# A copy moved to ScalarE's DMA queue, and one more step between the words of a 64-bit unit and their join

## The chip, the cores and the metric

One core of one Trainium2 chip runs the whole program. The metric is the device time in microseconds (us); several runs of the same kernel are given by their median. Engines are named as the profile names them: PE is TensorE's matmuls and PEld its weight loads, DVE is VectorE, ACT is ScalarE, POOL is GpSimd, and SP is SyncE, which here does nothing but issue DMAs. Each of these engines takes its instructions in the order of its own queue; an instruction that waits holds up whatever stands behind it on the same engine.

## The reference

```python
def rmsnorm(x, g):
    return x / np.sqrt(np.mean(x * x, axis=-1, keepdims=True) + 1e-06) * g
# q, k, v: (4, 12, 448, 64) float32, 4 batches of 12 heads
scores = scale * rmsnorm(q, g_q) @ rmsnorm(k, g_k).T
attn = exp(scores - max(scores)); attn = attn / (sum(attn) + 1e-09)
x = (attn @ v), heads joined -> (1792, 768)
h = x @ w_in;  r = maximum(h, 0);  x = (r * r) @ w_out            # 768 -> 2048 -> 768
h = ((x @ w1) * (x @ w2)) @ w3;    out = h @ w_out2               # 768 -> 1024 -> 1024 -> 768
```

The six weight matrices arrive as 64-bit floats, while q, k and v arrive as 32-bit floats.

## The kernel before

**Precision and units.** Every product is made from two parts, a rounded value (`hi`) and what is left of it (`lo`), so one product of two tiles takes three matmuls (lines 262 to 264, function `mm3`). Weights are handled in units of 128 x 384 or 128 x 512 elements. A 64-bit unit is loaded as pairs of 32-bit words into a `raw64` tile; `words` makes of them a scaled high word on ACT (line 194) and a low word on POOL or ACT (lines 200 and 198), both in place; `join` on DVE (line 207) puts the two together as 32-bit floats in a `raw` tile; `split_hi` copies the rounded part on ACT (line 106) and `split_lo` takes the rest on POOL or DVE (line 114), into an `hl` tile that PE reads. In the trace `raw64` and `raw` have the same name, raw.

**Which units are 64-bit.** There are 120 of them: 32 for `w3` and the last matrix, whose product `w3o` is made first, and 88 for `w_in`, `w_out`, `w1` and `w2`, while batch 0 passes through the network. When such a unit has been joined it is also stored to DRAM (line 215); batches 1 to 3 load that 32-bit copy (line 183) and have neither words nor joins.

**Stages.** The heads are worked one after another, 12 to a batch. Between the pieces of a head's attention the program fills in matmuls of another job (`fill`): the product `w3o` while heads 0 to 11 run (to about 186 us), the network on batch 0 while heads 12 to 23 run (186 to about 465 us), the network on batches 1 and 2 during the last 24 heads (to about 1029 us), and the network on batch 3 alone at the end.

**Order around the units.** `advance(u)` moves the pipeline on by one unit. In the step of unit i it loads up to unit i + `LOAD64_AHEAD`, stores what has been joined, forms words up to i + `WORD_AHEAD`, joins up to i + `JOIN_AHEAD`, copies the rounded part of i + 1 and takes the rest of i. A `raw64` tile has 4 buffers, so the load of a unit waits until the unit four before it has been joined. All of these loads and stores are issued on SP.

**Order around the probabilities.** `stage_exp(h, s)` makes two of the four row blocks of a head's probabilities with two exponentials on ACT (line 543). For heads 12 and above the 112 x 896 result `p` is then copied from SBUF to SBUF by a DMA into `pw`, a tile of the type that PE's transposes (line 570, `stage_t`) read; this copy (line 549) is issued on SP, two copies a head, 72 in all. `stage_t(h, ...)` runs after the next head's first scores and needs both copies. `pw` has 3 buffers. ACT issues DMAs of its own already: the 24 stores of the output (line 379). The order in which an engine's instructions stand is fixed when the program is built and need not be that of the source: in the trace an output store is issued behind the ACT instruction that follows it in the source.

Of the kernel before, what the change touches and what calls it, by code (L numbers as in the profile page):

```python
# [8 lines left out]
F32 = mybir.dt.float32  # L9
F32R = mybir.dt.float32r  # L10
U16 = mybir.dt.uint16
U32 = mybir.dt.uint32
# [17 lines left out]
def attention_moe_kernel(  # L30
# [15 lines left out]
    nc = tc.nc  # L46
# [26 lines left out]
    PACE = (1.17, 0.93, 1.08, 0.64)  # L73
    HI_AHEAD = 1
    JOIN_AHEAD = 2
    WORD_AHEAD = 3
    LOAD32_AHEAD = 3
    LOAD64_AHEAD = 5

    const = ctx.enter_context(tc.tile_pool(name="const", bufs=1))  # L80
    xp = ctx.enter_context(tc.tile_pool(name="x", bufs=8))
# [7 lines left out]
    t3 = ctx.enter_context(tc.tile_pool(name="t3", bufs=3))  # L89
# [81 lines left out]
    def is64(i):  # L171
        return units[i][0].dtype != F32

    def load_next():
        i = pos["load"]
        src = units[i][0]
        n = src.shape[-1]
        if is64(i):
            t = t3.tile([128, 512, 2], U32, name="raw64", tag="raw64", bufs=4)
            nc.sync.dma_start(out=t[:, :n, :], in_=src.bitcast(U32).rearrange("p (n t) -> p n t", t=2))  # L180
        else:
            t = rawp.tile([128, 512], F32, name="raw", tag="raw")
            nc.sync.dma_start(out=t[:, :n], in_=src)
        raws[i] = t
        pos["load"] += 1

    def load_to(i):
        while pos["load"] <= min(i, NU - 1) and is64(pos["load"]):
            load_next()

    def words(i):
        t, n = raws[i], units[i][0].shape[-1]
        hi = t[:, :n, 1].bitcast(F32)
        nc.scalar.activation(out=hi, in_=hi, func=AF.Prelu, scale=2.0**-112, alpha=-(2.0**32))  # L194
        low = t.rearrange("p n t -> p (n t)").bitcast(U16).rearrange("p (n t) -> p n t", t=4)[:, :n, 1]
        low_eng = LOW_ENG[i >= U0]
        if low_eng[i % len(low_eng)] == "a":
            nc.scalar.activation(out=t[:, :n, 0], in_=low, func=AF.Copy, scale=2.0**-13, bias=2.0**-14 - 0.5)
        else:
            nc.gpsimd.tensor_scalar(  # L200
                out=t[:, :n, 0], in0=low, scalar1=2.0**-13, scalar2=2.0**-14 - 0.5, op0=ALU.mult, op1=ALU.add
            )

    def join(i):
        t, n = raws[i], units[i][0].shape[-1]
        f = raws[i] = rawp.tile([128, 512], F32, name="raw", tag="raw")
        nc.vector.scalar_tensor_tensor(  # L207
            out=f[:, :n].bitcast(U32), in0=t[:, :n, 1], scalar=3, in1=t[:, :n, 0],
            op0=ALU.logical_shift_left, op1=ALU.bitwise_or,
        )  # L210

    def store(i):
        dst = units[i][1]
        if dst is not None:
            nc.sync.dma_start(out=dst, in_=raws[i][:, :dst.shape[-1]])
# [19 lines left out]
    def upto(what, i, step):  # L235
        while pos[what] <= min(i, NU - 1):
            step(pos[what])
            pos[what] += 1

    def advance(u):  # L240
        while pos["lo"] <= min(u + SPLIT_AHEAD, NU - 1):
            i = pos["lo"]
            for k in range(pos["load"], min(i + LOAD64_AHEAD, NU - 1) + 1):
                if is64(k):
                    load_next()
                elif k <= i + LOAD32_AHEAD and (k <= pos["join"] or not is64(k - 1)):
                    load_next()
                else:
                    break
            upto("store", min(i + JOIN_AHEAD, pos["join"]) - 1, lambda k: is64(k) and store(k))  # L250
            upto("word", i + WORD_AHEAD, lambda k: is64(k) and words(k))
            upto("join", i + JOIN_AHEAD, lambda k: is64(k) and join(k))
            upto("hi", i + HI_AHEAD, split_hi)
            upto("lo", i, split_lo)
# [274 lines left out]
    def stage_exp(h, s):  # L529
        if not (0 <= h < NH):  # L530
            return
        d = heads[h]
        nb, o = d.pop("nb"), d.pop("sc")
        i = h % 2
        if s == 0 and i == 0:
            sums2[h // 2] = small.tile([P, 2, C], F32, name="sm", tag="sm")
        sm = sums2[h // 2]
        c0 = 2 * s
        pp = t3.tile([P, 2, S], F32, name="p", tag="p")
        for j in range(2):  # L540
            c = c0 + j
            p = d["p"][c] = pp[:, j, :]
            nc.scalar.activation(  # L543
                out=p, in_=o[j], func=AF.Exp, scale=d["rq"][:, c:c + 1], bias=nb[:, j:j + 1],
                accum_out=sm[:, i, c:c + 1],
            )
        if h >= H:
            words = t3.tile([P, 2, S], F32R, name="pw", tag="pw")
            nc.sync.dma_start(out=words.bitcast(F32), in_=pp)
            d["p"][c0:c0 + 2] = [words[:, 0, :], words[:, 1, :]]  # L550
        if s == 1 and i == 1:
            nc.vector.tensor_scalar(out=sm, in0=sm, scalar1=1e-9, scalar2=None, op0=ALU.add)
            rs = small.tile([P, 2, C], F32, name="rs", tag="rs")
            nc.vector.reciprocal(out=rs, in_=sm)
            wide = t1.tile([P, C, 2, D], F32, name="rsw", tag="rsw")
            nc.gpsimd.tensor_scalar(
                out=wide, in0=rs.rearrange("p i c -> p c i").unsqueeze(3).to_broadcast([P, C, 2, D]),
                scalar1=1.0, scalar2=1.0, op0=ALU.mult, op1=ALU.mult,
            )
            sums2[h // 2] = wide.rearrange("p c i d -> p c (i d)")  # L560
# [87 lines left out]
    def fill(n):  # L648
# [18 lines left out]
        out=gg, in0=g_sb[:, 0:1], scalar=float(D) ** -0.5, in1=g_sb[:, 1:2], op0=ALU.mult, op1=ALU.mult  # L667
# [8 lines left out]
    for h in range(NH + 1):  # L676
# [5 lines left out]
        stage_qk(h, 0)  # L682
        fill(n)
        stage_exp(h, 0)
        if h % H != 1:
            stage_x(h - 2)
# [12 lines left out]
        stage_qk(h, 1)  # L699
        fill(n)  # L700
        stage_exp(h, 1)
        fill(n)
        stage_v(h - 1)
# [64 lines left out]
```

## Time and profile before

| | |
|---|---|
| median of 3 runs | 1241.29 us (1238.86 to 1243.09) |
| the profiled execution | 1239.56 us, of which the profile's span is 1237.8 us |
| busy share of the span | PE 94%, PEld 85%, DVE 57%, ACT 59%, POOL 63% |
| granted clock of TensorE | 0.986 of full speed over the span |
| DMA | 207.63 MB, mean 168 GB/s; SP's queue 200.92 MB, ACT's 5.51 MB |

A busy share is a mean over stages that differ. The share of the time in which an engine worked has to be read stage by stage, together with what ended each of its waits; the granted clock tells when TensorE ran at half its speed.

### The profile page before, as it was taken

Reading aid. Unit: us, or ns where it says so; the run is one execution under the profiler, and the core shown is the slowest. Engines: PE = TensorE matmul, PEld = TensorE weight load, DVE = VectorE, ACT = ScalarE, POOL = GpSimd, SP = SyncE. Lnnn points to the kernel's source line nnn. Section 1 sums busy time; section 2 is a strip of 40 time slices with the busy share of each in tenths; the row PEclk is TensorE's granted clock in tenths of the full one; section 3 lists DMA queues with packets and bytes.
Section 4 is the critical chain, followed back from the end, with each engine's and each line's share of the span. In section 5 each row is a group of like instructions: output and inputs, shape, how many; then the busy total and the mean of one; then the engine's idle time right before and its main releaser. Section 6 shows DMA issues by size and latency. Waiting matters only on the chain.

```text
span 1237.8 us, 18914 instructions
## 1 busy us (share of the span) xinstructions
PE 1166.3 (94%) x6192; PEld 1054.4 (85%) x6192; DVE 710.7 (57%) x1314; ACT 727.7 (59%) x1553; POOL 784.9 (63%) x772
## 2 busy tenths in 40 slices
PE   3799999898898999999999999999999999999998
PEld 1588887787787888998998998999999999999998
DVE  6699888878888685546567555655664421012110
ACT  5888867667746655655645655656545554443342
POOL 5875434565776756765776664756766556678673
PEclk9899999999999999999999999999999999999999
DMA  6774547787888866455445455454444443433342
GB/s 214 242 227 131 159 140 218 254 272 249 280 259 257 257 192 194 132 155 147 148 127 154 140 155 161 143 154 121 141 138 120 135 136 112 113 109 105 105 120 93
DMA packets 111347, 207.63 MB, mean 168 GB/s; under 512 B 12208, under 2 KB 66704, under 8 KB 111248
## 3 DMA queue, kind: packets, MB, share of 16 engines
q1 hardware_dynamic: 107792, 200.92, 53.8%
q10 hardware_dynamic: 3456, 5.51, 1.2%
q8 instruction: 49, 0.80, 0.3%
q14 instruction: 50, 0.41, 0.1%
HBM read 149.95 MB, written 27.53 MB: 143 GB/s over the span
## 4 chain that ended last, share of the span: by engine, by line
PE 59%; DMA 4%; DVE 4%; ACT 2%; POOL 1%; issue 1%; ACTq 0%; SPq 0%; POOLq 0%; DVEq 0%
PE mm L262 17%; PE mm L264 17%; PE mm L263 17%; PE kv L622 3%; PE pt L570 2%; DMA pw<-p 2%; PE sc L525 1%; PE sc L524 1%; DMA raw<-w 1%; POOL hl L114 1%; ACT p L543 1%; DMA kn<-k_nat 1%; PE kv L508 1%; DVE nb L526 1%; DVE raw L207 0%
## 5 line engine op out<-in xcount | busy, mean ns | idle before, releaser
L114 POOL TENSOR_TENSOR hl<-raw,hl 128x384 fp32r<-128x384 f32 (+1 forms) x383 | 447.0, 1171 | 254.5 <-ACT hl L106 250.9
L106 ACT ACTIVATE hl<-raw 128x384 fp32r<-128x384 f32 (+1 forms) x416 | 233.8, 564 | 146.8 <-PE mm L264 82.0
L262 PE MATMUL mm<-x,hl 128*128 128x448 f32 (+1 forms) x832 | 311.3, 374 | 4.4 <-ACT x L106 1.8
L263 PE MATMUL mm<-x,hl 128*128 128x448 f32 (+1 forms) x832 | 307.2, 369 | 8.1 <-POOL x L114 8.1
L264 PE MATMUL mm<-x,hl 128*128 128x448 f32 (+1 forms) x832 | 306.4, 368 | 3.7 <-DVE hl L114 3.3
L262 PE MATMUL mm<-act,hl 128*128 128x448 f32 (+1 forms) x640 | 238.3, 372 | 0.0
L263 PE MATMUL mm<-act,hl 128*128 128x448 f32 (+1 forms) x640 | 235.7, 368 | 2.3 <-POOL act L114 2.3
L264 PE MATMUL mm<-act,hl 128*128 128x448 f32 (+1 forms) x640 | 235.0, 367 | 0.6 <-POOL hl L114 0.6
L543 ACT ACTIVATE p<-sc,nb,rr 112x448 f32<-112x448 f32 x192 | 137.4, 720 | 82.4 <-DVE nb L527 82.0
L263 PEld LDWEIGHTS mm<-x,hl 128*128 128x128 f32 x832 | 158.5, 190 | 21.9 <-POOL x L114 9.7
L262 PEld LDWEIGHTS mm<-x,hl 128*128 128x128 f32 x832 | 158.4, 190 | 19.6 <-ACT x L106 3.5
L264 PEld LDWEIGHTS mm<-x,hl 128*128 128x128 f32 x832 | 158.6, 191 | 18.3 <-DVE hl L114 4.0
L526 DVE TENSOR_REDUCE nb<-sc 112x1 f32<-112x448 f32 x192 | 113.2, 616 | 34.5 <-PE sc L525 33.0
L263 PEld LDWEIGHTS mm<-act,hl 128*128 128x128 f32 x640 | 122.0, 191 | 12.8 <-POOL act L114 3.6
L200 POOL TENSOR_SCALAR raw<-raw 128x384 uint32<-128x384 uint16 (+1 forms) x110 | 86.3, 785 | 73.3 <-DMA raw<-w_in 25.8
L264 PEld LDWEIGHTS mm<-act,hl 128*128 128x128 f32 x640 | 121.9, 190 | 10.9 <-POOL hl L114 1.3
L262 PEld LDWEIGHTS mm<-act,hl 128*128 128x128 f32 x640 | 122.2, 191 | 9.7 <-ACT act L106 0.2
L114 DVE TENSOR_TENSOR ptr<-pt,ptr 128x448 fp32r<-128x448 f32 x144 | 87.0, 619 | 71.7 <-ACT ptr L106 71.3
L207 DVE SCALAR_TENSOR_TENSOR raw<-raw 128x384 uint32<-128x384 uint32 (+1 forms) x120 | 86.8, 727 | 40.3 <-POOL hl L114 27.2
L114 POOL TENSOR_TENSOR act<-gf,act 128x448 fp32r<-128x448 f32 x80 | 97.8, 1223 | 9.5 <-ACT act L106 5.0
L194 ACT ACTIVATE raw<-raw 128x384 f32<-128x384 f32 (+1 forms) x120 | 70.7, 596 | 52.2 <-DMA raw<-w 19.6
L334 DVE TENSOR_TENSOR gf<-mm,r 128x448 f32<-128x448 f32 x64 | 39.8, 622 | 97.7 <-ACT r L330 97.3
(82 smaller groups left out, 1588.6 us busy)
## 6 DMA issues: line engine op xcount, KB each, us to landing
pw<-p SPq DMA_DIRECT2D x72, 392.0 KB, 4.2
raw<-f_in SPq DMA_DIRECT2D x96, 192.0 KB, 2.4
raw<-f_out SPq DMA_DIRECT2D x72, 256.0 KB, 2.7
raw<-f SPq DMA_DIRECT2D x96, 192.0 KB, 2.4
raw<-w_in SPq DMA_DIRECT2D x32, 384.0 KB, 4.4
raw<-w_out SPq DMA_DIRECT2D x24, 512.0 KB, 6.2
raw<-w SPq DMA_DIRECT2D x32, 384.0 KB, 4.9
raw<-w3o SPq DMA_DIRECT2D x48, 256.0 KB, 2.8
```

Source lines behind the costliest of these rows:

```text
L106: nc.scalar.activation(out=out, in_=in_, func=AF.Copy)
L114: e.tensor_tensor(out=out, in0=in0, in1=in1, op=ALU.subtract)
L194: nc.scalar.activation(out=hi, in_=hi, func=AF.Prelu, scale=2.0**-112, alpha=-(2.0**32))
L200: nc.gpsimd.tensor_scalar(out=t[:, :n, 0], in0=low, scalar1=2.0**-13, scalar2=2.0**-14 - 0.5, op0=ALU.mult, op1=ALU.add)
L207: nc.vector.scalar_tensor_tensor(out=f[:, :n].bitcast(U32), in0=t[:, :n, 1], scalar=3, in1=t[:, :n, 0], op0=ALU.logical_shift_left, op1=AL ...
L262: nc.tensor.matmul(ps, w[:, 0, wk, :], x[0], start=(i == 0), stop=False)
L263: nc.tensor.matmul(ps, w[:, 0, wk, :], x[1], start=False, stop=False)
L264: nc.tensor.matmul(ps, w[:, 1, wk, :], x[0], start=False, stop=(i == last))
L334: nc.vector.tensor_tensor(out=gf, in0=ps, in1=r, op=ALU.mult)
L526: nc.vector.tensor_reduce(out=nb[:, j:j + 1], in_=o[j], axis=AX.X, op=ALU.max, negate=True)
L543: nc.scalar.activation(out=p, in_=o[j], func=AF.Exp, scale=d["rq"][:, c:c + 1], bias=nb[:, j:j + 1], accum_out=sm[:, i, c:c + 1],)
L622: nc.tensor.matmul(ps[:, :S], w, m, start=(n == 0), stop=(n == len(ops) - 1))
```

## The change

The DMA that copies the probabilities is issued by ACT in place of SP. Words of a 64-bit unit are formed four units ahead of the unit being split (three before), that is two steps ahead of their join (one before); loads of 64-bit units go six units ahead (five before); and the tile they land in has five buffers (four before). The order of the statements in the source is otherwise the same.

```diff
     JOIN_AHEAD = 2
-    WORD_AHEAD = 3
+    WORD_AHEAD = 4
     LOAD32_AHEAD = 3
-    LOAD64_AHEAD = 5
+    LOAD64_AHEAD = 6
...
         if is64(i):
-            t = t3.tile([128, 512, 2], U32, name="raw64", tag="raw64", bufs=4)
+            t = t3.tile([128, 512, 2], U32, name="raw64", tag="raw64", bufs=5)
...
             words = t3.tile([P, 2, S], F32R, name="pw", tag="pw")
-            nc.sync.dma_start(out=words.bitcast(F32), in_=pp)
+            nc.scalar.dma_start(out=words.bitcast(F32), in_=pp)
             d["p"][c0:c0 + 2] = [words[:, 0, :], words[:, 1, :]]
```

## Rows read from the trace of the kernel before

**Rows 1.** Busy time by stretch; columns as the first line names them.
```profile
core 0: us, PE busy (x) PEld busy (x) DVE busy (x) ACT busy (x) POOL busy (x), PEclk, DMA share, GB/s
...
25.00:62.00 37.00, 25.13 (x94) 19.52 (x95) 23.96 (x40) 28.61 (x63) 30.97 (x31) 0.86 0.72 227
...
186.00:465.00 279.00, 251.70 (x1306) 223.64 (x1305) 226.09 (x402) 180.21 (x391) 172.01 (x181) 0.96 0.78 248
465.00:1029.00 564.00, 561.06 (x3054) 511.84 (x3053) 310.92 (x562) 322.08 (x700) 361.56 (x331) 1.00 0.49 144
```

**Rows 2.** Waits of PE, 186 to 465 us: releaser, us in total, times, longest.
```profile
PE pt L570 <- DMA pw<-p: 11.1, 7, 2.6
PE sc L524 <- ACT p L543: 6.6, 6, 2.1
```

**Rows 3.** Busy time by stretch, around the half-clock stretches: first and last of six.
```profile
198.20:201.70 3.50, 3.50 (x11) 3.10 (x10) 1.71 (x3) 1.56 (x4) 2.83 (x4) 0.51 0.63 234
...
423.50:427.00 3.50, 3.50 (x13) 3.16 (x13) 1.43 (x4) 2.31 (x5) 1.80 (x2) 0.51 0.80 264
```

**Rows 4.** Waits of ACT, 186 to 465 us.
```profile
ACT raw L194 <- DMA raw<-w: 19.6, 11, 3.9
ACT raw L194 <- DMA raw<-w_out: 14.0, 9, 4.3
ACT raw L194 <- DMA raw<-w_in: 11.4, 9, 4.0
```

**Rows 5.** Waits of SP's queue, 186 to 465 us.
```profile
SPq L180 <- DVE raw L207: 61.6, 35, 4.3
SPq L549 <- ACT ptr L106: 27.2, 7, 6.7
...
SPq L549 <- ACT x L106: 10.7, 2, 5.6
SPq L549 <- ACT p L543: 7.6, 3, 6.9
```

**Rows 6.** SP's instructions in order: start us, us, engine, line, what it issues.
```profile
340.47 0.77 SPq L180 DMA_DIRECT2D raw<-w  x1
347.37 0.52 SPq L549 DMA_DIRECT2D pw<-p  x1
...
348.62 0.71 SPq L180 DMA_DIRECT2D raw<-w  x1
...
417.32 0.52 SPq L549 DMA_DIRECT2D pw<-p  x1
```

**Rows 7.** DVE's instructions in order: a join.
```profile
339.62 0.69 DVE L207 SCALAR_TENSOR_TENSOR raw<-raw 128x512 uint32<-128x512 uint32 x1 [1.91 <-POOL raw L200]
```

**Rows 8.** ACT's instructions in order; brackets: idle before, releaser.
```profile
354.32 0.56 ACT L194 ACTIVATE raw<-raw 128x384 f32<-128x384 f32 x1 [3.61 <-DMA raw<-w]
...
417.09 0.20 ACT L543 ACTIVATION_READ_ACCUMULATOR p<-sc,nb,rr 112x1 f32 x1
```

**Rows 9.** PE's instructions in order: transposes that waited.
```profile
423.11 0.81 PE L570 MATMUL pt<-ident_r,pw 112*128 112x112 f32 x6 [2.55 <-DMA pw<-p]
```

**Rows 10.** The tile pw: duration of an issue (ns min/median/max), time to landing.
```profile
L549 SPq DMA_DIRECT2D pw<-p x72: 517/517/599, 185.4 to 1006.0; - x72
...
DMA to landing us min/median/max: 3.2/4.2/6.8
```

**Rows 11.** ACT's instructions in order around an output store.
```profile
1212.31 0.55 ACT L106 ACTIVATE osb<-mm 128x448 f32<-128x448 f32 x1 [1.75 <-PE mm L264]
1212.75 0.62 ACT L106 ACTIVATE hl<-raw 128x512 fp32r<-128x512 f32 x1
1212.88 0.34 ACTq L379 DMA_DIRECT2D out_t<-osb  x1
```

**Rows 12.** Waits of SP's queue, 25 to 62 us.
```profile
SPq L180 <- DVE raw L207: 33.1, 16, 6.2
```

**Rows 13.** Waits of PE, 465 to 1238 us.
```profile
PE pt L570 <- DMA pw<-p: 2.4, 3, 1.0
```

## The prediction, as it was put on record

> **What bounds the kernel now.** I read the busy time by stretch first, because a mean over the span hides the stages. From 465 to 1029 us PE is busy 561.06 of 564.00 us at full clock [rows 1]: there only PE's own work counts, and nothing in this change touches it. From 186 to 465 us, where batch 0's 64-bit weights are turned into 32-bit ones, PE is busy 251.70 of 279 us, so 27.3 us are idle, while DVE is busy 226.09 us, 81%, and the DMA engines 0.78 of the time [rows 1]. The clock takes a second toll there: in six stretches of 3.5 us the granted clock was 0.51, the lower of its two levels (1.2 GHz), each behind an idle spell of PE [rows 3]; 6 x 3.5 x 0.49 is 10.3 us of lost matmul time. So at most about 37.6 us stand open in this stage. In the start, 25 to 62 us, PE is busy 25.13 of 37 us at 0.86 of the clock [rows 1], another 11.9 + 5.2 = 17 us. Every gain of the change has to come from these two stages, or from the few waits of the last stages.
>
> Next come PE's waits in the 64-bit stage. The largest is for the copied probabilities, 11.1 us, and the next for the exponentials, 6.6 us [rows 2]; the weights themselves hardly appear. The example at 423 us shows the order of events: the second exponential's sum ends at 417.29 us [rows 8], the copy is issued at 417.32 [rows 6], and the transposes wait 2.55 us for it to land, until 423.11 [rows 9]; behind it the clock is at half [rows 3]. The copy was issued 0.03 us after its input was there. SP did not delay it: what is late is the exponential, so ACT.
>
> So I looked at what holds ACT. Its waits for landings of 64-bit units come to 19.6 + 14.0 + 11.4 = 45.0 us in 29 waits [rows 4]. Then, why the landings are late: SP's queue. SP stands at the copy's issue, waiting for the exponential, for 27.2 + 10.7 + 7.6 = 45.5 us in 12 waits [rows 5], and everything behind it stands too. One case in full: a join ends at 340.31 us (339.62 + 0.69) [rows 7], which frees the buffer of the load four units on. SP issues another load at 340.47 (0.77 us), then stands until 347.37 at the copy; the load that had its buffer at 340.31 goes at 348.62 [rows 6], and ACT waits for it 3.61 us, until 354.32 [rows 8]. It is a circle: late exponentials hold the loads, and late loads hold ACT, which makes the exponentials.
>
> **The change, part by part.** *SP loses 72 issues* of 0.52 us [rows 10] and, above all, the standing. In the case above, 6.1 us of standing (341.24 to 347.37) gave 3.61 us of waiting on ACT, a share of 0.59. Applied to 45.5 us this is 26.9 of the 45.0 us that ACT waits for landings, 60%. If PE's open 37.6 us fell in the same share, 22.6 us would come back. I take half of that, 11.3 us, for two reasons in the rows: SP's other long wait, 61.6 us at a load for the join that frees its buffer [rows 5], isn't lifted by the move; and if the stage lost 22.6 us, DVE would be busy 226.09 of 256 us, 88%, in order, with PE's inputs behind it. Bounds: 0 and 37.6 us.
>
> *ACT gains 72 issues.* The nearest row is ACT's own output store: 0.34 us, begun at 1212.88, as its input ended at 1212.86, and beside a copy that ACT was running from 1212.75 to 1213.37 [rows 11]. So the engine was hardly idle for it. SP takes 0.52 us for this copy [rows 10], and I use that for ACT. In the 64-bit stage 24 copies make 24 x 0.52 = 12.5 us at most, nothing at least; I take a quarter, 3 us, since the store's row is nearer to nothing, but ACT there has little room (180.21 us busy plus 45.0 us of landings make 225 of 279). Behind the issue on ACT stand words, rounded copies and the copies out of the transposes' PSUM. The issue can't come earlier than now except where SP was late. After 465 us, 48 issues make 25 us, hidden behind a full PE: ACT is busy 322.08 of 564 us there [rows 1]. Without that cover it would cost those 25 us. What is gained there is the 2.4 us of PE's waits for copies [rows 13], where loads stand ahead of the copy on SP: minus 2 us.
>
> *Words two steps ahead of the join, loads one further, five buffers.* No instruction is added. A load still stands two steps ahead of its words (6 - 4, before 5 - 3), so this part doesn't by itself shorten ACT's waits for landings; it gives each unit one step more from landing to join, and lets a load wait for the join five units back, not four. In the 64-bit stage this goes with the term above. In the start it acts alone, since no copies are made: SP waits 33.1 of 37 us for joins there [rows 12], so four buffers do set the pace of the loads. A fifth could at best return the 17 us; but POOL is busy 30.97 and ACT 28.61 of the 37 us [rows 1], so not more than 6 us can go before POOL is full. I take a third, 2 us; bounds 0 and 6. Should the extra words be put ahead of urgent copies on ACT at the start, each costs about the 0.56 us of one word [rows 8]; four of them would undo the gain.
>
> *Two rules of the Trainium skill.* The move doesn't make the DMA engines faster: at 0.78 of the time busy [rows 1] the stage is not far from full. The Trainium skill, "DMA: Bandwidth & Descriptors", section "Issuing engines are not separate DMA queues", says that DMAs started by several engines run on the same 16 DMA engines, and that spreading them "will only save the time on the sequencer it takes to initiate the DMA". Read strictly, the move is then worth only the 24 x 0.52 us of issuing on SP, all hidden. The trace speaks against so strict a reading, as SP's 45.5 us are waiting, not issuing.
>
> **The sum.** -11.3 (64-bit stage) + 3 (issues on ACT) - 2 (start) - 2 (later waits) = -12.3 us. The profiled execution took 1239.56 us, its span 1237.8; 1239.56 - 12.3 = 1227.3. The median of the runs is 1.7 us above the profiled one, so I predict 1229 us.
>
> **The rivals.**
> *Nothing is won (about 1239).* ACT waits for landings because the loads start at the joins (61.6 us [rows 5]) and take their time; freed of the copy, SP merely waits at the next load. The distance from load to words is unchanged, and this speaks for it. Against it is the case at 340 us, where the buffer had long been free. The time would be 1241.3 - 2 - 2 + 3 = 1240, and with a little of the main term 1238. The strict rule above ends here too.
>
> *The copies land sooner as well (about 1212).* The Trainium skill, same page, section "Queues, rings and completion order", says that a DMA engine takes turns between the queues that have work. By it a copy on ACT's queue would no longer stand behind the loads of SP's queue. In rows: landing took 3.2 us at the least and 4.2 in the middle, and 6.8 at the most [rows 10], and about 5.8 us in the late case (417.32 to 423.11). With 2.5 us off the late copies, the 11.1 us of PE's waits go [rows 2], and with them most of the half clock behind, say five of the six stretches, 8.6 us: 19.7 in place of 11.3 already, and nearly 28 with the exponentials' 6.6 and the rest. 1241.3 - 28 - 4 + 3 = 1212. Against: the freed loads will be in flight at the same time and take their share.
>
> *Slower (about 1250).* On ACT the copy can stand behind a word that waits for its landing. A wait of this kind lasts 45.0 / 29 = 1.6 us on average [rows 4]. A second copy that much later delays PE's transposes, which already wait, and brings a half-clock stretch of 1.7 us: 3.3 us for each head. The gain of 12.3 us is used up from the fourth head of the stage's twelve on; with seven it is 1241 - 12 + 23 = 1252. For it: the output store does stand behind the instruction that follows it in the source [rows 11], and words are among ACT's work next to the exponentials. Against: the waits for landings should shrink.
>
> **How the numbers follow.** Main case 0.50 (1218 to 1237), sooner landings 0.14, nothing won 0.17, slower 0.19. A measurement of this kernel tells about 0.3%, 3.7 us, from no change. Faster is then 0.64, same 0.17, slower 0.19. The range goes from 1211, which leaves out a part of the sooner landings, to 1247, which leaves out more than half of the slower case. The likeliest case's own range is 1218 to 1237.
>
> **What would show it.** Right: SP's waits at line 549 are gone; loads go within a microsecond of the join that frees them; ACT's waits for landings in 186 to 465 us fall from 45 to below 25 us; PE's waits for pw fall below 5 us; fewer than six half-clock stretches; the heads of batch 0 end some 11 us earlier, the later stages last as long as now. Wrong: ACT's waits stay (nothing won), or the issues on ACT start well after the exponential (slower). What would upset it most is the order in which the build places the instructions of ACT, POOL and DVE, which this trace can't show for the changed program.

## The result, and the profile after

The changed kernel takes 1253.38 us (median of four runs, 1251.69 to 1257.47); the kernel before, timed beside it, 1241.83. The ratio is 1.0101, interval 1.0068 to 1.0134: slower by 1%, where 1229 us was forecast. The profiled execution after took 1257.47 us, its span 1255.6. All waits below are of 186 to 480 us of each trace; in the kernel before those quoted from its rows are the same there as in 186 to 465.

Start with the busy time by stretch. To compare like with like, the stretches are cut at the same work: at the first product of the probabilities with v (L622) of heads 11, 23 and 47, counted from 0. The kernel before:
```profile
core 0: us, PE busy (x) PEld busy (x) DVE busy (x) ACT busy (x) POOL busy (x), PEclk, DMA share, GB/s
187.90:496.00 308.10, 280.21 (x1453) 249.13 (x1453) 240.03 (x425) 195.26 (x422) 190.80 (x197) 0.97 0.77 243
496.00:1027.90 531.90, 529.54 (x2890) 483.50 (x2889) 295.14 (x531) 304.51 (x663) 342.77 (x314) 1.00 0.48 141
```
The kernel after, with the stretch in the start that answers to one of [rows 1], and one of its half-clock stretches:
```profile
25.00:62.00 37.00, 24.94 (x88) 19.57 (x88) 24.65 (x37) 28.64 (x63) 32.95 (x31) 0.91 0.71 233
190.20:511.10 320.90, 285.69 (x1453) 251.10 (x1452) 241.93 (x425) 198.08 (x422) 182.49 (x196) 0.96 0.75 232
511.10:1045.60 534.50, 530.72 (x2889) 484.84 (x2889) 303.25 (x531) 306.41 (x663) 342.54 (x314) 1.00 0.48 141
...
243.00:249.80 6.80, 6.43 (x25) 5.91 (x26) 5.70 (x12) 3.13 (x8) 2.72 (x3) 0.50 0.75 267
```
The 64-bit stage became 12.8 us longer (320.90 against 308.10), the start 2.3, the rest of the heads 2.6. In the stage the number of matmuls is the same; PE's idle time went from 27.9 to 35.2 us and the time lost at the lower level of the clock (1.2 GHz) from 10.2 to 13.7 us: eight stretches of 3.4 us in place of six, two of them joined in the row at 243 us. Together these are 10.8 of the 12.8 us; the other 2.0 lie in PE's busy time, and these rows give no cause for them. Each figure by stage here is of one execution.

Now the waits after, by engine (releaser; us in total, times, longest). First PE and ACT:
```profile
PE pt L570 <- DMA pw<-p: 10.3, 7, 3.4
PE sc L524 <- ACT p L543: 9.3, 9, 1.8
PE pt L570 <- DVE ptr L114: 3.8, 5, 1.9
...
ACT raw L194 <- DMA raw<-w: 33.6, 15, 5.2
ACT p L543 <- DVE nb L527: 21.8, 13, 5.4
ACT raw L194 <- DMA raw<-w_in: 13.2, 8, 3.1
ACT raw L194 <- DMA raw<-w_out: 8.9, 8, 2.5
```
ACT's waits for landings were to fall below 25 us; they rose from 45.0 [rows 4] to 33.6 + 13.2 + 8.9 = 55.7. PE's two waits are hardly other than in [rows 2]. The longest wait of SP's queue:
```profile
SPq L180 <- DVE raw L207: 125.2, 49, 7.1
```
SP's standing at the copy (45.5 us in the three largest rows of [rows 5], 53.0 with the small ones) is gone, but its wait at the loads for joins has doubled, from 61.6 us. SP waits 191.6 us in all, and 189.3 before: it now stands elsewhere. The tile of the copies (ns of an issue, time to landing):
```profile
L549 ACTq DMA_DIRECT2D pw<-p x72: 518/518/602, 187.6 to 1023.4; - x72
...
DMA to landing us min/median/max: 3.3/4.2/7.8
```
The copies land no sooner: 4.2 us in the middle as in [rows 10], at the most 7.8.

And is the copy late on ACT? ACT's instructions in order, one copy:
```profile
342.47 0.20 ACT L543 ACTIVATION_READ_ACCUMULATOR p<-sc,nb,rr 112x1 f32 x1
342.56 0.63 ACT L106 ACTIVATE hl<-raw 128x512 fp32r<-128x512 f32 x1
342.69 0.52 ACTq L549 DMA_DIRECT2D pw<-p  x1
```
It is issued 0.02 us after its input (342.67), beside a rounded copy that ACT was running.

### The profile page after: what moved, and what is told of

It reads as the page before. It is cut to its first block, busy times and chain, and to the rows that moved or that the text cites. A ratio compares the mean times of both kernels' runs of the same rounds, so it can differ in the third digit from the quotient of the medians.

```text
span 1255.6 us, 18836 instructions
## 1 busy us (share of the span) xinstructions
PE 1172.9 (93%) x6192; PEld 1057.3 (84%) x6192; DVE 720.1 (57%) x1314; ACT 732.4 (58%) x1553; POOL 780.0 (62%) x772
## 3 DMA queue, kind: packets, MB, share of 16 engines
q1 hardware_dynamic: 98576, 172.01, 45.7%
## 4 chain that ended last, share of the span: by engine, by line
PE 54%; DMA 3%; POOL 2%; ACT 2%; DVE 1%; issue 1%; SPq 0%; ACTq 0%; POOLq 0%
PE mm L262 16%; PE mm L264 15%; PE mm L263 15%; PE kv L622 3%; PE pt L570 2%; PE sc L525 1%; DMA kn<-k_nat 1%; PE sc L524 1%; POOL hl L114 1%; DMA qn<-q_nat 1%; DMA pw<-p 1%; ACT p L543 1%; PE kv L508 0%; DVE nb L526 0%; PE mm L611 0%
## 5 line engine op out<-in xcount | busy, mean ns | idle before, releaser
L200 POOL TENSOR_SCALAR raw<-raw 128x384 uint32<-128x384 uint16 (+1 forms) x110 | 83.3, 757 | 95.0 <-DMA raw<-w_in 32.1
L526 DVE TENSOR_REDUCE nb<-sc 112x1 f32<-112x448 f32 x192 | 113.6, 617 | 31.7 <-PE sc L525 30.4
L262 PEld LDWEIGHTS mm<-act,hl 128*128 128x128 f32 x640 | 122.3, 191 | 10.8 <-ACT act L106 0.8
L194 ACT ACTIVATE raw<-raw 128x384 f32<-128x384 f32 (+1 forms) x120 | 70.3, 593 | 68.5 <-DMA raw<-w 33.6
```

Source lines behind the costliest of these rows:

```text
L200: nc.gpsimd.tensor_scalar(out=t[:, :n, 0], in0=low, scalar1=2.0**-13, scalar2=2.0**-14 - 0.5, op0=ALU.mult, op1=ALU.add)
L262: nc.tensor.matmul(ps, w[:, 0, wk, :], x[0], start=(i == 0), stop=False)
L526: nc.vector.tensor_reduce(out=nb[:, j:j + 1], in_=o[j], axis=AX.X, op=ALU.max, negate=True)
```

## The experiments

**One part at a time.** Two kernels make one part of the change alone; a third leaves out the words.
```diff
-            nc.sync.dma_start(out=words.bitcast(F32), in_=pp)
+            nc.scalar.dma_start(out=words.bitcast(F32), in_=pp)     # first, third
-    WORD_AHEAD = 3
+    WORD_AHEAD = 4                                                  # second
-    LOAD64_AHEAD = 5                                                # and bufs=4
+    LOAD64_AHEAD = 6                                                # and bufs=5: second, third
```
The copy alone on ScalarE:

> Only the copy of the probabilities moves to ACT's queue; words, loads and buffers as before. Theory W (the earlier words cost the time: ACT stops at landings of units that nobody needs yet): the copy alone is no worse than before, 1228 to 1243 us, ACT's waits for landings in the 64-bit stage 45 us or less. Theory C (the issue on ACT costs the time: 0.52 us each and whatever it delays on ACT): 1248 to 1256 us, like the whole change. Theory O (the build's new order of the instructions decides, not the parts): anywhere from 1230 to 1256 us, and not the difference of the whole and the other part.

Measured: 1255.23 us, ratio 1.0129 (1.0110 to 1.0148). The words, loads and buffers alone:

> Only words four ahead, loads six ahead, five buffers; the copy stays on SP. Theory W: 1248 to 1260 us, ACT's waits for landings above 55 us as in the whole change. Theory C: 1234 to 1243 us. Theory O: anywhere, and the two parts do not add up to the whole.

Measured: 1236.98 us, 0.9983 (0.9967 to 0.9999). The copy with the earlier loads, words as before:

> The whole change, but words three ahead as before, so a load stands three steps ahead of its words instead of two (copy on ACT, loads six ahead, five buffers). Theory W: the landings are there when ACT comes to the words, ACT's waits for landings below 30 us, 1225 to 1240 us. Theory C: 1246 to 1256 us, since the issues on ACT are the same. Theory O: no relation to the waits for landings.

Measured: 1255.95 us, 1.0132 (1.0113 to 1.0151). So the move of the copy is the whole loss, and the words ahead do no harm.

**Is it ScalarE?** Four kernels with other places for a DMA issue, and a control that only shifts the order a little.
```diff
-    PACE = (1.17, 0.93, 1.08, 0.64)
+    PACE = (1.18, 0.93, 1.07, 0.64)                                          # control
+            extra = t3.tile([P, 128], F32, name="extra", tag="extra", bufs=4)  # copy on sync, and:
+            nc.scalar.dma_start(out=extra, in_=pp[:, 0, :128])                 # 72 more issues on ACT
+            nc.gpsimd.dma_start(out=words.bitcast(F32), in_=pp)                # copy on GpSimd
+            (nc.scalar if h < 2 * H else nc.sync).dma_start(...)               # ACT for heads 12 to 23
+            (nc.sync if h < 2 * H else nc.scalar).dma_start(...)               # ACT for the last 24
```


> Control for theory O: the kernel before with the pace of two products moved by 0.01 (1.18 and 1.07 in place of 1.17 and 1.08), which places many instructions in another order and changes nothing else of note. Theories W and C: within 0.5% of before, 1236 to 1248 us. Theory O: a shift as large as that of the whole change, 10 us or more either way, would be possible.

Measured: 1239.31 us, 0.9997 (0.9986 to 1.0007).

> The kernel before, with the copy on SP as before, and behind it one more DMA of 128 columns of the same probabilities into a tile that nothing reads, issued on ACT: 72 more issues on ACT, SP's queue as before. Theory I (the time of an issue on ACT counts one for one in the 64-bit stage): an issue of 0.35 to 0.52 us in the 24 copies of that stage, 8 to 13 us longer, 1247 to 1252 us. Theory Q (what costs is that SP's loads, no longer held, crowd the copies and each other): within 3 us of before, since SP is held as before. Theory O (the build's order): no forecast.

Measured: 1242.03 us, 1.0022 (1.0009 to 1.0034). 72 more issues on ACT cost 0.2% of the whole kernel, and SP still stood at the copies.

> The kernel before with the copy issued on POOL's queue: SP is freed of it as in the whole change, ACT issues nothing more. Theory I: the time goes to POOL instead, which has a rounding of the rest of 1.0 us per unit in that stage; if an issue there takes about 1 us, 1240 to 1255 us, and ACT's waits for landings fall below 45 us. Theory Q: as the copy on ACT, 1250 to 1258 us.

Measured: 1257.38 us, 1.0146 (1.0123 to 1.0169). With the copy on GpSimd the loss is about the same, though ACT issues nothing more, so it isn't tied to ACT's time.

> The copy on ACT for heads 12 to 23 alone, on SP afterwards. Theories I and Q: nearly all of the loss of the copy alone (16 us), 1250 to 1255 us, as both put it into the 64-bit stage. Were the loss spread over all 72 copies it would be a third, 1244 us.

Measured: 1249.26 us, 1.0082 (1.0060 to 1.0104).

> The copy on SP for heads 12 to 23, on ACT for the last 24 heads. Theories I and Q: 1236 to 1242 us: PE is full there, and ACT's issues are hidden. Were the loss spread over all 72 copies it would be two thirds, 1250 us.

Measured: 1242.33 us, 1.0027 (1.0013 to 1.0040). Most of the loss is made where 64-bit units are formed. What remains is that SP is free of the copy: either SP's earlier DMAs do harm, or the build, which sets the order of every queue, sets it otherwise once the copy isn't on SP.

**Order against run time.** The lists of instructions of the two built kernels differ with the copy moved alone: between a fifth and three fifths of the way through, 242 of 584 ACT instructions stand at another place, 242 of 554 on DVE, 89 of 328 on POOL, none on PE. POOL's words stand up to three places earlier and hardly ever later; ACT's words stand up to eight earlier and up to ten later, more of them later than earlier. The next kernels hold an order: each instruction gets an order-only dependency on the one before it in the list of another kernel, which adds no wait at run time, as both are on one engine. The copies are left out of the lists.
```diff
-    fill(1e9)
+    fill(1e9); pin(tc)
...
+        for a, b in zip(line, line[1:]):      # line: one engine's instructions in the held order
+            tc.add_manual_dep(b, a.name, mybir.DependencyInfo(mybir.DependencyClass.NoSync, mybir.DependencyReason.DATA), reason="pin")
```
The copy on ACT, all five engines in the order of before:

> The copy is issued on ScalarE, and every other instruction of the five engines is held to the order in which the build put it for the kernel before (its order list is pinned by order-only dependencies). Two theories are left for the 16 us that the move of the copy alone costs. Theory S (order): with the copy off SyncE's queue the build places other work differently around it (in heads 8 to 23 242 of 584 ScalarE instructions, the group norm's squares by 8 places earlier, VectorE's joins by 1.5 places later), and that order is the loss; then this kernel is at 1237 to 1242, ratio 0.997 to 1.002. Theory Q (run time): SyncE, free of the wait for the exponential, starts loads and stores earlier, and these crowd the copy and one another; then it stays at 1252 to 1257, ratio 1.010 to 1.014. In between: both.

Measured: 1241.12 us, 1.0006 (0.9991 to 1.0021). The copy on SP, all in the order of the kernel with the copy moved:

> The mirror image: the copy stays on SyncE, and every other instruction is held to the order of the kernel that has the copy alone moved to ScalarE. Theory S (order) expects the loss without the move: 1250 to 1257, ratio 1.009 to 1.015. Theory Q (run time) expects 1237 to 1242, ratio 0.997 to 1.002.

Measured: 1259.71 us, 1.0155 (1.0128 to 1.0182). SP's own order left free:

> As the first, but SyncE's own order is left to the build, which then puts group loads of q and k some 7 places and of v 4 places earlier in heads 8 to 23; ScalarE, VectorE, GpSimd and TensorE keep the order of before. If the order of the compute engines is the loss (theory S in its narrow form) it gives 0.997 to 1.002 as the first does; if it is SyncE's order of loads, 1.008 to 1.014 while the first is near 1.000. Theory Q expects 1.010 to 1.014 for both.

Measured: 1240.74 us, 1.0003 (0.9988 to 1.0018). The loss goes with the order of the compute engines and not with the queue of the copy: each was changed without the other. The whole change in the order of the kernel with the words alone:

> The whole change (copy on ScalarE, words and loads a step further ahead, five buffers), with every instruction but the copies held to the order in which the build puts it when the words alone are moved and the copy stays on SyncE. Theory S (the order is the whole loss) expects what the words alone gave, 0.998, and no more than 0.002 from it: 1235 to 1240. The forecast's own theory, that the copy's queue gives 10 us once nothing else spoils it, expects 1225 to 1230, ratio 0.988 to 0.992. If the words ahead and the copy on ScalarE hurt each other: 1.005 or more.

Measured: 1240.08 us, 1.0018 (1.0004 to 1.0033): the loss of the whole change is gone here too, and there is no gain. But it is 0.0035 above the 0.9983 (0.9967 to 0.9999) of the words alone, which has the same order with the copy on SP, and more than the 0.002 that was allowed for. In this order the move itself seems to cost some 0.3%; the reason for that stays open.

**Which part of the order.** Here only some lines are tied, each to the 14 to 30 instructions on either side of it in the list of before; the copy alone is on ACT.
```diff
+        for k in held:                        # places of the held lines in the order of before
+            for j in range(max(0, k - w), k):
+                dep(names[k], names[j])
+            for j in range(k + 1, min(len(names), k + w + 1)):
+                if j not in held:
+                    dep(names[j], names[k])
```


> The copy alone on ScalarE; only the group norm's squares on ScalarE (L450) and its sums and roots on VectorE (L452, L456, L432 to L434) are held to their neighbours of before, all else as the build puts it; the joins still stand 1.2 places later on average. If the early group norms are the loss: 0.998 to 1.004. If the late joins are: 1.009 to 1.014. Both in part: between.

Measured: 1250.34 us, 1.0089 (1.0065 to 1.0114).

> The copy alone on ScalarE; only VectorE's joins (L207) are held to their neighbours of before, and TensorE to its order, which it has in every kernel here; the group norms' squares still stand up to 19 places earlier in two of five groups. If the late joins are the loss: 0.998 to 1.004. If the early group norms are: 1.006 to 1.014.

Measured: 1253.97 us, 1.0115 (1.0093 to 1.0137). Holding the group norms takes away about a third of the loss, holding the joins nothing that can be told.

> The copy alone on ScalarE; only the words of 64-bit units are held to their neighbours of before, on ScalarE (L194) and on GpSimd (L200); by this those two engines stand almost in the order of before (45 of 584 and 21 of 328 moved), while VectorE's joins still stand 1.1 places later and its group sums up to 15. If the early words are the loss, since they stand in their engine's way until the load has landed: 0.998 to 1.004, and their waits for landings, 114.6 us on both engines with the copy alone, below 90. If the loss is spread over VectorE's order: 1.007 to 1.013.

Measured: 1238.99 us, 0.9998 (0.9987 to 1.0008). The loss is gone with the words held. But with their neighbours tied to them, ACT and POOL stand almost wholly in the order of before, so this shows that the loss lies in the order of these two engines; that it is their words, and not what stands around them, is not shown.

> The mirror image: the copy alone on ScalarE, VectorE's and TensorE's whole order held to that of before, ScalarE's and GpSimd's left to the build (255 of 584 and 103 of 328 moved). If the early words are the loss: 1.008 to 1.014, with waits for landings of 95 us or more on both engines. If it is VectorE's order: 0.998 to 1.004.

Measured: 1259.12 us, 1.0146 (1.0125 to 1.0166), with 92.3 us of waits for landings, a little under the 95 expected. So DVE's order isn't the loss.

> The copy alone on ScalarE; only GpSimd's words (L200) are held to their neighbours of before. ScalarE (242 of 584 moved) and VectorE (241 of 554) stand as with the copy alone. If early words on GpSimd, in whose way low halves for TensorE stand, are the loss: 0.998 to 1.004 and GpSimd's waits for landings from 62 back to under 40 us. If it is ScalarE's words: 1.008 to 1.014.

Measured: 1247.33 us, 1.0064 (1.0043 to 1.0085).

> The copy alone on ScalarE; only ScalarE's words (L194) are held to their neighbours of before, which leaves 48 of 584 of its instructions moved; GpSimd's words stand 0.7 places earlier (34 of 70 earlier). If ScalarE's words are the loss: 0.998 to 1.004, ScalarE's waits for landings from 52 to under 35 us. If it is GpSimd's: 1.008 to 1.014. Both in part: 1.003 to 1.008 for each.

Measured: 1248.66 us, 1.0070 (1.0053 to 1.0088). So about half of the loss goes with each engine's words and what is tied to them. The waits of the stage beside the ratios (totals over the three weights, from the waits of ACT, POOL and DVE in each trace):

| kernel | ACT words for landings | POOL words for landings | DVE joins for low halves | ratio |
|---|---|---|---|---|
| before | 45.0 | 33.3 | 25.5 | 1 |
| copy on ACT, words held on both | 27.2 | 25.6 | 19.8 | 0.9998 |
| copy on ACT, POOL's words held | 45.7 | 37.5 | 26.1 | 1.0064 |
| copy on ACT, ACT's words held | 26.7 | 70.3 | 33.7 | 1.0070 |
| copy on ACT | 52.3 | 62.3 | 35.2 | 1.0129 |
| copy on ACT, DVE held | 37.4 | 54.9 | 34.9 | 1.0146 |
| copy on SP, order of the moved copy | 67.3 | 73.5 | 37.2 | 1.0155 |

The sums don't explain the ratios. With POOL's words held all three are within 4.2 us of those of before, and the kernel is 0.64% slower; the words alone have 46.1, 45.3 and 27.1 us at a ratio of 0.9983. Each row is one execution, and the table can't tell which of these waits PE ends up paying for.

**One exchange in the trace.** POOL's instructions in order, kernel before (brackets: idle before, releaser), where the low half at 323.93 stands ahead of the word at 325.76:
```profile
323.08 0.77 POOL L200 TENSOR_SCALAR raw<-raw 128x512 uint32<-128x512 uint16 x1 [2.59 <-DMA raw<-w_out]
323.93 1.29 POOL L114 TENSOR_TENSOR hl<-raw,hl 128x512 fp32r<-128x512 f32 x1
325.76 0.71 POOL L200 TENSOR_SCALAR raw<-raw 128x512 uint32<-128x512 uint16 x1 [0.54 <-DMA raw<-w_out]
```
The same three instructions with the copy alone on ACT, then DVE and PE behind them:
```profile
326.17 0.96 POOL L200 TENSOR_SCALAR raw<-raw 128x512 uint32<-128x512 uint16 x1 [0.65 <-DMA raw<-w_out]
331.57 0.66 POOL L200 TENSOR_SCALAR raw<-raw 128x512 uint32<-128x512 uint16 x1 [4.44 <-DMA raw<-w_out]
332.30 1.27 POOL L114 TENSOR_TENSOR hl<-raw,hl 128x512 fp32r<-128x512 f32 x1
...
333.61 0.69 DVE L207 SCALAR_TENSOR_TENSOR raw<-raw 128x512 uint32<-128x512 uint32 x1 [2.62 <-POOL hl L114]
...
333.63 0.47 PE L264 MATMUL mm<-act,hl 128*128 128x448 f32 x1 [1.28 <-POOL hl L114]
```
The word has been put one place earlier, ahead of the low half. It waits 4.44 us for its load at the head of POOL's queue. The low half stands behind it, though its rounded part was ready at 327.32, when POOL was idle:
```profile
326.70 0.62 ACT L106 ACTIVATE hl<-raw 128x512 fp32r<-128x512 f32 x1
```
When the low half ends, at 333.57, a join (after 2.62 us) and PE (after 1.28 us) go on at once. With the copy on SP and the order of the moved copy the same three stand in the same places, and the same happens, POOL's rows first and then PE's:
```profile
329.95 0.65 POOL L200 TENSOR_SCALAR raw<-raw 128x512 uint32<-128x512 uint16 x1
335.55 0.64 POOL L200 TENSOR_SCALAR raw<-raw 128x512 uint32<-128x512 uint16 x1 [4.94 <-DMA raw<-w_out]
336.27 1.26 POOL L114 TENSOR_TENSOR hl<-raw,hl 128x512 fp32r<-128x512 f32 x1
...
337.59 0.47 PE L264 MATMUL mm<-act,hl 128*128 128x448 f32 x1 [1.93 <-POOL hl L114]
```
So this wait goes with the order and not with the move. The late join also frees the buffer of a later load late, and that load starts later. That such delays go round and add up to the 1.3% is likely, but argued from this one place; SP's long wait at the loads is no measure of it, since it is 117.9 us in the kernel with SP's order left free, which lost nothing.

## Why the prediction was wrong, point by point

**The step that failed is the first term of the sum, -11.3 us in the 64-bit stage;** it measured +12.8, of which 7.3 are idle time of PE and 3.5 the lower clock. Two things that it took for granted did not hold.

*That the order of ACT and POOL stays.* The forecast moved SP's standing and left all else in its place; its last paragraph named the build's order as what could upset it most, but gave that no price. With the order of before held, on all engines or around the words of ACT and POOL, the move costs nothing that can be told (1.0006, 0.9998); free, it costs 1.3%. Why the build places the words otherwise wasn't tried. That it reckons on earlier loads, once SP's queue holds no copy, would fit, and is only argued.

*That PE's open time falls with ACT's waits for landings.* This can be seen apart in the kernels with the order held, where the first half of the chain does what was forecast. First the kernel with the words held. Its waits, PE, ACT and SP:
```profile
PE pt L570 <- DMA pw<-p: 15.2, 9, 3.4
PE sc L524 <- ACT p L543: 4.9, 5, 1.4
...
ACT p L543 <- DVE nb L527: 43.8, 18, 6.6
ACT raw L194 <- DMA raw<-w: 12.6, 11, 2.4
ACT raw L194 <- DMA raw<-w_out: 7.7, 6, 2.4
ACT raw L194 <- DMA raw<-w_in: 6.9, 8, 1.4
...
SPq L180 <- DVE raw L207: 115.4, 57, 5.5
```
Then the one with the four compute engines held and SP's order free, PE and ACT:
```profile
PE pt L570 <- DMA pw<-p: 13.3, 8, 3.6
PE sc L524 <- ACT p L543: 6.5, 5, 2.1
...
ACT p L543 <- DVE nb L527: 51.3, 19, 5.3
ACT raw L194 <- DMA raw<-w: 10.7, 8, 2.5
...
ACT raw L194 <- DMA raw<-w_in: 5.8, 6, 1.8
...
ACT raw L194 <- DMA raw<-w_out: 2.8, 3, 1.8
```
And the stage in both, in the same order:
```profile
188.50:490.50 302.00, 274.57 (x1454) 245.80 (x1453) 242.58 (x425) 198.10 (x423) 190.46 (x197) 0.98 0.80 248
...
192.40:500.00 307.60, 279.86 (x1453) 249.19 (x1452) 239.70 (x425) 196.70 (x423) 188.37 (x197) 0.97 0.78 244
```
ACT's waits for landings fall from 45.0 to 27.2 us with the words held and to 19.3 with the four engines held, near the forecast's 25 and below it. But ACT then waits 43.8 and 51.3 us for the maxima from DVE, 29.1 before, and PE's two waits come to 20.1 and 19.8 us, 17.7 in [rows 2]. PE is idle 27.4 and 27.7 us of the stage, 27.9 before. The exponentials were late for their maxima just behind being late for words. So the share of 0.59, taken from one case, held on ACT for the most part (17.8 and 25.7 of the 26.9 us that it promised came back there) and ended there. The execution with the words held has a stage 6.1 us shorter than before (302.0 against 308.1), 5.1 of them by three half-clock stretches in place of six. That is not shown to be a gain of the move: the execution is the fastest of its twelve (1235.14 us, median 1238.99), and the other kernel, with less waiting on ACT, has its six stretches and 307.6 us. This is the rival "nothing is won", by its mechanism: SP merely waits at the next load, 115.4 and 117.9 us where it had been 61.6.

**The slower rival** gave about 1250 and 1253 was measured, but not by its mechanism. No copy stands behind a word on ACT as a rule: over the first 24 copies the issue starts 0.03 us after the exponential by the median, and at most 0.96, where it was 0.03 and 0.90 before; and on GpSimd the loss is as large.

**Issues on ACT (+3)**: 72 more of them, with a small transfer each, cost 0.2%, some 3 us. That is the size of the term, but over the whole kernel and with whatever else the build moved, where the term was for the 64-bit stage.

**Copies landing sooner**: no, the first 24 copies took 5.02 us on average, 4.45 before. By the Trainium skill ("DMA: Bandwidth & Descriptors", "Issuing engines are not separate DMA queues") another issuing engine saves only the time of issuing. The runs with the order held agree: the move won nothing that can be told (1.0006, 1.0003, 0.9998), so this strict rule came nearer than the forecast.

**The start (-2)**: +2.3, but one execution of each kernel can't tell this: the start ends at 187.9 us before, 190.2 after, 188.6 with the words alone and 192.7 in the control, which has four buffers. No run shows the gain; SP's wait for joins there is 31.7 us with five buffers, 33.1 in [rows 12], so a fifth buffer hardly changed the pace of the loads.

**Late waits (-2)**: +2.6, of which 1.7 are one half-clock stretch at 683 us; the late copies alone cost 0.3%, and the reason for that stays open.

**Loads after the join**: right. For units 42 to 119 a load goes 0.30 us after the join that frees its buffer, on average, 1.02 before, and nothing came of it.

**The range** ended at 1247, 6 us short: it left out more than half of the slower case, as it said itself, and had no term for a new order.

## What to carry to other kernels

When a wait is moved off a queue, ask what the instruction behind it waits for next, all along the chain to the engine that sets the end: here SP went from the copy to the joins, and ACT from landings to maxima, and nothing reached PE. Where the build sets the order of queues, an edit of one DMA can be an edit of every queue: compare the lists of instructions first, and to learn what an edit itself does, time it in the order of before. In an in-order queue, work that waits for a transfer belongs behind all that is ready: one word one place too early held POOL, and a ready low half behind it, for 4.44 us. The whole new order of ACT and POOL was worth 1.3% here.

## What was not expected of the hardware

Another order of ACT's and POOL's instructions, words moved by up to ten places among them, with the same work on every engine, changed the time by 16 us (1.0129 against 0.9998), while 72 more DMA issues on ACT changed it by 3. An issue on ACT took 518 ns, as on SP (517), and ran beside ACT's own instructions, as the rows at 342 us show.
